# When the next tile's weights are split: the split of w1 put ahead of the second product, that of w2 one part of the first product earlier

## The chip, the cores and the metric

One of the eight cores of a Trainium2 chip runs the kernel. The metric is the device time of one execution in microseconds (us); of several executions the median counts. TensorE (PE in the rows, its weight loads PEld) multiplies matrices, VectorE (DVE), ScalarE (ACT) and GpSimd (POOL) work element by element, and SyncE (SP) issues transfers. Each engine executes its own instructions in the order in which the program gives them, and waits for others by semaphores.

## The reference

```python
def reference(r, k, v, w, u, moe..., moe2...):
    attn = _attn_ref(r, k, v, w, u)      # linear attention with a decay w, 4 x 8 heads, 768 steps, 48 wide
    x = attn as (3072 tokens, 384)
    # mixture of experts: each token goes to the expert with the largest logit
    logits = x @ w_gate + modality_bias[modality_id]
    e_idx = argmax(logits);  gate_w = softmax(logits)[e_idx]
    for e in range(8):
        h = maximum(x[mask] @ w1[e], 0)              # 384 -> 1024
        out[mask] = gate_w[mask] * (h @ w2[e])       # 1024 -> 384
    # a last network, the same for all tokens
    h = maximum(maximum(x @ w1, x @ w2), x @ w3)     # 384 -> 768
    return h @ w_out                                 # 768 -> 384
```

The decay w is drawn between 0.80 and 0.95. The modality bias is drawn with a spread of 0.5 for two modalities, so most tokens of a modality go to one expert.

## The kernel before, in words

The kernel has three stages. First the attention, over 24 tiles of 128 tokens, with the routing of each tile behind it. Then `first_block`: the expert layer, over 13 tiles of 256 tokens that are sorted by expert (the list `seq`: tiles 0 and 1, an extra tile X for what is left of the first expert, then tiles 2 to 11; `s` counts 0 to 12, and `EARLY` is 2, the place of X). Then `second_block`: the last network, on 512 tokens at a time.

All products are done with numbers in two parts. A value `a` is split into `ah`, its rounding to fp32r, and `al = a - ah`, and a product is the sum of three matmuls: high by high, low by high and high by low. In `mm3` these are lines 1143, 1144 and 1145; the third is the one that reads the low part of the weights (`w1l` or `w2l`). A split is one ACT instruction (line 502, the cast to `w1h` or `w2h`) and one subtraction (line 504) on DVE; for parts 1, 3, 4 and 6 of w2 the subtraction is on POOL (`W2_DVE = (0, 2, 5, 7)` names those on DVE).

One tile of the expert layer goes like this:

- `g1(q)`, q = 0 to 3: a quarter of the first product, 18 matmuls over 256 tokens for two blocks of 128 columns of `h` (three slices of the depth, three matmuls each), into one PSUM bank. ACT then writes `hh` (line 1156), DVE `hl` (line 1157). Blocks 0 to 3 use the weights that `split_w1` makes in parts 0 to 2, blocks 4 to 7 those of parts 3 to 5; each part is one of the three slices of the depth.
- behind each `g1(q)`, for s above 2, `split_w2` makes parts 2q and 2q+1 of w2, for the second product of the same tile.
- `reload(..., 1)`: SP loads the next tile's w2 into `w2r`, if that tile has another expert. It waits until the splits have read `w2r`.
- `next_columns`: PE transposes the next tile's tokens, ACT writes `xh` and DVE `xl` (lines 1136 and 1137).
- `rows_of` and `ids_of`: POOL clears buffers and issues the indirect transfers that fetch the tokens of the tile after the next.
- `g2(q)`, q = 0 and 1: the second product, 48 and then 24 matmuls; of the eight slices of the depth the last two come last. ACT copies each result to `raw` (line 1172). Behind each of the two, `split_w1` makes three parts of w1 of the next tile.
- `reload(..., 0)` loads w1 of the tile after the next, and `keep` writes `raw` to memory (SP, lines 1092 and 1176).

Between these calls `vw(n)` puts n steps of another job, which splits the weights of the last network: DVE lines 528 to 556, ACT lines 524 and 549, POOL lines 552 and 559 (`vh`, `vl`, `voh`, `vol`), loads on SP by line 517. `manual_schedule` leaves each engine with the order in which the code calls.

Line 495 is elsewhere: `check_w` counts over the 128 partitions those in which every decay w lay between 0.7 and 1.4 (a matmul with ones), and sets `badw` if the count is too small; `badw` then leads to a general attention that computes all again. Partitions 0 to 15 and 64 to 79 hold padding, which is set to 1.0.

Of the kernel before, what the change touches and what calls it, by code (L numbers as in the profile page):

```python
# [15 lines left out]
ALU = mybir.AluOpType  # L16
# [32 lines left out]
def kernel(ctx: ExitStack, tc: tile.TileContext, rkw_t, v_t, vrk, u, modality, w_gate, bias, w1, w2, v1, v2,  # L49
                              v3, v_out, out):  # L50
    nc = tc.nc
    PE, DVE, ACT, POOL, SP = nc.tensor, nc.vector, nc.scalar, nc.gpsimd, nc.sync
    B, NC, _, D, _, HP, _ = rkw_t.shape
# [16 lines left out]
    EARLY = 2  # L70
# [26 lines left out]
    lgps = lgpool.tile([128, 512], F32, name="lgps")  # L97


    def ct(shape, dt, name):  # L100
        return const.tile(shape, dt, name=name)
# [38 lines left out]
    badw = ct([128, 1], F32, "badw")  # L140
# [171 lines left out]
    def settle(a, b):  # L312

        POOL.memset(places[:, a:b], 0)
# [40 lines left out]
    def plan(es):  # L355
# [37 lines left out]
        end = t2("end")  # L393
        DVE.tensor_tensor_scan(out=end, data0=zero8, data1=co, initial=cgs, op0=ALU.add, op1=ALU.add)
        checked = check_w()
        next(checked)
        yield "X"
# [88 lines left out]
    def check_w():  # L486

        fl = small.tile([128, 1], F32, tag="fl", name="fl")
        DVE.tensor_reduce(out=fl, in_=flag, axis=AX.XY, op=ALU.max)
        good = small.tile([128, 1], BF16, tag="good", name="good")  # L490
        DVE.tensor_scalar(out=good, in0=fl, scalar1=0.0, scalar2=None, op0=ALU.is_equal)
        yield
        PE.matmul(lgps[:, 272:273], lhsT=ones_bf, rhs=good, start=True, stop=True)
        yield
        DVE.tensor_scalar(out=badw, in0=lgps[:, 272:273], scalar1=2.0 * D, scalar2=None, op0=ALU.is_lt)
        yield
        DVE.tensor_copy(ctl[:, 62:63], badw)

# [770 lines left out]
    ex = Experts()  # L1269
# [41 lines left out]
    def ids_of(j):  # L1311
        for half in range(2):
            ex.gather_ids(T[j]["oi"][half], idxm[:, 2 * j + half:2 * j + half + 1])

    def rows_of(s):
        ex.room(s)
        for half in range(2):
            ex.gather(s, half)
# [10 lines left out]
    def go(n):  # L1329
        for _ in range(n):  # L1330
            next(work, None)

    def until(what):
        for got in work:
            if got == what:
                return

    def first_block(vw):

        seq = T[0:EARLY] + [X] + T[EARLY:]  # L1340
        tile_of = list(range(EARLY)) + [None] + list(range(EARLY, N))
        def next_columns(nx):
            for q in range(2):
                ex.x_part(nx, q)
        for s, cur in enumerate(seq):
            nx = seq[s + 1] if s <= N - 1 else None
            for q in range(4):
                if s == 0 and q < 2:
                    continue
                if s == 0:  # L1350
                    ex.g1((q,), lambda: go(FIRST_GO[2 * q - 3]))
                else:
                    ex.g1((q,))
                if s > EARLY:
                    ex.split_w2((2 * q, 2 * q + 1))
                    vw(V_OPS[3] if s == EARLY + 1 else V_OPS[4][q])
                elif s < EARLY:
                    if s == 0:
                        if q == 2:
                            ex.split_w2((6, 7), W2_FIRST)  # L1360
                        go(FIRST_GO[2 * q - 2])
                    if s:
                        go(6)
                if s == EARLY:
                    vw(V_OPS[2])
            if s == EARLY - 1:
                until("X")
                settle(NG, NTILE)
                for half in range(2):
                    ex.gather_ids(X["oi"][half], idxx[:, half:half + 1])  # L1370
                rows_of(X)
                until("rows")
                ids_of(EARLY)
                rows_of(T[EARLY])
                until("end")
                ids_of(EARLY + 1)
            if s >= EARLY and nx:
                ex.reload(tile_of[s + 1], 1)
            if not nx:
                second_start()  # L1380
            if nx and nx is not X:
                next_columns(nx)
            if s >= EARLY and s + 2 <= N:
                rows_of(seq[s + 2])
            if s >= EARLY and s + 3 <= N:
                ids_of(tile_of[s + 3])
            for q in range(2):
                ex.g2(cur, (q,))
                if nx is X and q == 0:
                    next_columns(X)  # L1390
                if s >= EARLY:
                    if nx:
                        ex.split_w1(range(3 * q, 3 * q + 3))
                elif s == 0:
                    go(6)
                if EARLY - 1 <= s:
                    vw(V_OPS[s] if s <= EARLY else V_OPS[6])
            if EARLY <= s + 1 <= N - 1:
                ex.reload(tile_of[s + 2], 0)
            if cur is not X:  # L1400
                ex.keep(cur, tile_of[s])
        m = maskx.rearrange("p (t a) -> p t a", a=2)[:, EARLY:]
        DVE.copy_predicated(oi_all.rearrange("p (t a) c -> p t a c", a=2)[:, EARLY:],
                            m.unsqueeze(3).to_broadcast([128, N - EARLY, 2, 2]),
                            oe.unsqueeze(1).to_broadcast([128, N - EARLY, 2, 2]))

    def second_start():
        ex.open_second(2 * TW)
        ex.x2(ex.fetch(0, 2 * TW))
# [52 lines left out]
    with tc.manual_schedule():  # L1462
        wes = ExitStack()
        ex.open_first(wes)
        e = NTILE

        hooks = {(13, "mid"): [chosen, bind(first_load, 0, 0)],
                 (14, "end"): [first_room],
                 (e - 2, "uterm"): [first_x, bind(ex.split_w1, (0, 1, 2))],
                 (e - 2, "late"): [bind(ex.split_w1, (3, 4, 5), "h")],  # L1470
                 (e - 1, "uterm"): [bind(ex.split_w1, (3, 4, 5), "l"), bind(ex.g1, (0,)),
                                    bind(ex.split_w2, (0, 1), W2_FIRST)],
                 (e - 1, "mid"): [bind(ex.split_w2, (2, 3), W2_FIRST)],
                 (e, "mid"): [bind(ex.g1, (1,), rest_of_routing)],
                 (e, "end"): [bind(ex.split_w2, (4, 5), W2_FIRST)]}
        for q in range(1, 7):
            hooks[(13 + q, "mid")] = [bind(first_load, q // 3 if q < 6 else 1, q if q < 3 else q - 3)]
        attention(hooks)
        pools["mm"] = pool(ctx, "mm", 4, space=PSUM)
        wres = pool(ctx, "wres", 1)  # L1480
        vh = [wres.tile([128, KD, F2], F32R, name=f"vh{i}") for i in range(3)]
        vl = [wres.tile([128, KD, F2], F32R, name=f"vl{i}") for i in range(3)]
        voh = wres.tile([128, KF2, DM], F32R, name="voh")
        vol = wres.tile([128, KF2, DM], F32R, name="vol")
        with ExitStack() as es:
            vw = v_stream(pool(es, "stage", 2))
            first_block(vw)
            second_block(vw)
        wes.close()
        rest()  # L1490
# [50 lines left out]
```

## Time and profile before

| | |
|---|---|
| time, median of 3 runs | 766.49 us (760.2 to 769.64) |
| the profiled execution | 770.97 us, its span 769.3 us, mean granted clock 0.948 |
| PE busy | 720.2 us (94%), PEld 642.9 us |
| DVE, ACT, POOL busy | 494.0 us (64%), 318.7 us (41%), 363.8 us (47%) |
| attention and routing, with the first expert tile | about 0 to 222 us |
| expert tiles from the first `raw` copy on | 222.3 to 450.4 us |
| last network | 450.4 to 769.3 us |

Busy shares are of the span. A matmul's duration in a row is longer than the distance to the next one, since matmuls are pipelined: of successive matmuls the difference of their start times tells what each costs.

### The profile page before, as it was taken

The numbers are of one execution on the slowest core, as the hardware profiler recorded it, in microseconds if no ns is written. First come the engines' busy times: TensorE is split into PE (matmuls) and PEld (weight loads), VectorE is DVE, ScalarE is ACT, GpSimd is POOL, SyncE is SP. The second block draws the span as 40 slices with busy tenths as digits, with TensorE's granted clock in tenths as the row PEclk, the third lists the DMA queues.
The fourth block names the chain that finished last, engine by engine and source line by source line (L and its number), as shares of the span: only waits on it lengthen the run. The fifth ranks groups of instructions, "written<-read, shape, count | busy, mean of one in ns | idle before, by whom it ended". The sixth has DMA issues, their size and how long they took to land.

```text
span 769.3 us, 13303 instructions
## 1 busy us (share of the span) xinstructions
PE 720.2 (94%) x4909; PEld 642.9 (84%) x4910; DVE 494.0 (64%) x929; ACT 318.7 (41%) x698; POOL 363.8 (47%) x388
## 2 busy tenths in 40 slices
PE   6899888889999999999999999999999999999991
PEld 3788767777899989999999987988988889889881
DVE  4899996996786998888888889424143142242320
ACT  5475645554333656566566633211212112122210
POOL 8699868898746667666764435110200101002011
PEclk8699989878599999999999999999999999999996
DMA  9899989993013322122235232020200200001000
GB/s 240 203 249 252 214 173 232 269 273 121 22 50 104 84 65 82 62 65 81 63 118 183 83 124 84 6 77 1 83 0 3 82 0 32 11 0 42 1 21 25
DMA packets 32383, 74.59 MB, mean 97 GB/s; under 512 B 5974, under 2 KB 19062, under 8 KB 32309
## 3 DMA queue, kind: packets, MB, share of 16 engines
q1 hardware_dynamic: 27508, 64.15, 30.5%
q0 software_dynamic: 4800, 9.49, 4.0%
q8 instruction: 41, 0.67, 0.4%
q14 instruction: 34, 0.27, 0.1%
HBM read 87.96 MB, written 14.38 MB: 133 GB/s over the span
## 4 chain that ended last, share of the span: by engine, by line
issue 37%; PE 30%; DVE 12%; DMA 8%; POOL 7%; ACT 2%; POOLq 0%; SPq 0%; DVEq 0%; ACTq 0%
DMA tq<-in_rkw_t_dram 6%; PE mm L1145 6%; PE mm L1144 5%; PE mm L1143 5%; PE yb L805 4%; POOL out_dram L1228 3%; DVE w1l L504 3%; PE mm L775 2%; PE yb L811 2%; DMA vt<-in_v_t_dram 1%; POOL w2l L504 1%; PE tp L788 1%; PE tp L706 1%; PE tp L859 1%; DMA w2r<-in_moe_w_dram 1%
## 5 line engine op out<-in xcount | busy, mean ns | idle before, releaser
L1208 DVE TENSOR_TENSOR w2r<-mm,w2r 128x512 f32<-128x512 f32 x72 | 49.7, 690 | 150.2 <-PE mm L1145 150.1
L1228 POOL DMA_INDIRECT out_dram<-w2r,oi_all x24 | 26.0, 1084 | 250.2 <-ACT w2r L1227 249.6
L1143 PE MATMUL mm<-w1h,vh 128*128 128x512 f32 x324 | 128.2, 396 | 0.9 <-DVE w2r L1208 0.9
L1145 PE MATMUL mm<-w1h,vl 128*128 128x512 f32 x324 | 128.2, 396 | 0.0
L1144 PE MATMUL mm<-w1l,vh 128*128 128x512 f32 x324 | 128.1, 395 | 0.0
L1145 PE MATMUL mm<-hh,w2l 128*128 128x256 f32 x312 | 89.3, 286 | 2.0 <-DVE w2l L504 1.0
L1144 PE MATMUL mm<-hl,w2h 128*128 128x256 f32 x312 | 88.5, 284 | 1.0 <-DVE hl L1157 1.0
L1143 PE MATMUL mm<-hh,w2h 128*128 128x256 f32 x312 | 89.2, 286 | 0.0
L1145 PE MATMUL mm<-xh,w1l 128*128 128x256 f32 x300 | 85.9, 286 | 2.2 <-DVE w1l L504 2.2
L1143 PE MATMUL mm<-xh,w1h 128*128 128x256 f32 x300 | 85.0, 283 | 0.0
L1144 PE MATMUL mm<-xl,w1h 128*128 128x256 f32 x300 | 84.8, 283 | 0.0
L1210 ACT CAST w2h<-w2r 128x512 fp32r<-128x512 f32 x36 | 22.3, 621 | 139.3 <-DVE w2r L1208 139.3
L1143 PEld LDWEIGHTS mm<-w1h,vh 128*128 128x128 f32 x324 | 60.9, 188 | 15.7 <-DVE w2r L1208 1.3
L1145 PEld LDWEIGHTS mm<-w1h,vl 128*128 128x128 f32 x324 | 60.9, 188 | 14.7
L1144 PEld LDWEIGHTS mm<-w1l,vh 128*128 128x128 f32 x324 | 60.9, 188 | 14.4
L504 POOL TENSOR_TENSOR w2l<-w2r,w2h 128x384 fp32r<-128x384 f32 x44 | 49.7, 1136 | 41.6 <-ACT w2h L502 39.1
L504 DVE TENSOR_TENSOR w1l<-w1r,w1h 128x512 fp32r<-128x512 f32 x66 | 51.8, 838 | 23.8 <-ACT w1h L502 23.7
L1145 PEld LDWEIGHTS mm<-hh,w2l 128*128 128x128 f32 x312 | 59.7, 191 | 3.9 <-DVE w2l L504 2.6
L805 PE MATMUL yb<-nat,am 128*128 128x56 f32 x384 | 53.1, 297 | 8.6 <-DVE lh L834 5.0
L1144 PEld LDWEIGHTS mm<-hl,w2h 128*128 128x128 f32 x312 | 59.7, 191 | 1.5 <-DVE hl L1157 1.4
L1145 PEld LDWEIGHTS mm<-xh,w1l 128*128 128x128 f32 x300 | 57.5, 192 | 4.1 <-DVE w1l L504 4.1
L1143 PEld LDWEIGHTS mm<-hh,w2h 128*128 128x128 f32 x312 | 59.8, 192 | 0.0
(252 smaller groups left out, 1728.0 us busy)
## 6 DMA issues: line engine op xcount, KB each, us to landing
w1r<-in_moe_w_dram SPq DMA_DIRECT2D x10, 1536.0 KB, 7.0
w2r<-in_moe_w_dram SPq DMA_DIRECT2D x10, 1536.0 KB
nat<-in_vrk_dram SPq DMA_DIRECT2D x24, 608.0 KB, 10.1
tq<-in_rkw_t_dram SPq DMA_DIRECT2D x46, 288.0 KB, 8.7
stg<-in_moe_w_dram SPq DMA_DIRECT2D x18, 384.0 KB, 3.1
vt<-in_v_t_dram SPq DMA_DIRECT2D x24, 192.0 KB, 6.6
x2t<-raw SPq DMA_DIRECT2D x12, 384.0 KB, 2.3
w1r<-x2t SPq DMA_DIRECT2D x12, 384.0 KB, 3.9
```

What stands on the lines that cost most here:

```text
L504: eng.tensor_tensor(out=lo, in0=src, in1=hi.bitcast(F32), op=ALU.subtract)
L706: PE.matmul(ps, lhsT=s["vt"][:, q, :], rhs=wgb[:, q].rearrange("p h e -> p (h e)"), start=(q == 0), stop=(q == KD - 1))
L775: PE.matmul(ps[o][:, p * 128:(p + 1) * 128], lhsT=s["kt"][q, p, :], rhs=s["rt"][q, p, :], start=True, stop=True)
L788: PE.transpose(out=ps[:, p * 128:(p + 1) * 128], in_=s["kt"][:, p, :], identity=ident)
L805: PE.matmul(yb[:, h * DV:(h + 1) * DV], lhsT=s["am"][:, 4 * (h % 2) + h // 2, :], rhs=s["v"][:, h, :], start=(h == 0), stop=(first and h = ...
L811: PE.matmul(yb[:, 2 * p * DV:(2 * p + 2) * DV], lhsT=s["rt"][:, p, :], rhs=sbd[i % 2][:, p, :], start=False, stop=(p == HP - 1))
L1143: PE.matmul(oc, lhsT=wh[:, kk, sl], rhs=xh[:, kk, :], start=first and kk == 0, stop=False)
L1144: PE.matmul(oc, lhsT=wh[:, kk, sl], rhs=xl[:, kk, :], start=False, stop=False)
L1145: PE.matmul(oc, lhsT=wl[:, kk, sl], rhs=xh[:, kk, :], start=False, stop=last and kk == nk - 1)
L1208: DVE.tensor_tensor(out=hv, in0=o, in1=hv, op=ALU.max)
L1210: ACT.copy(self.h2h[:, c, :], hv)
L1228: ins = POOL.indirect_dma_start(out=out[:, :], out_offset=bass.IndirectOffsetOnAxis(ap=ids[q][:, 0:1], axis=0), in_=ob, in_offset=None, bo ...
```

## The change

In `first_block` three lines move. For s above 2, `split_w2` of parts 0 and 1 is called ahead of `g1(0)`, and behind `g1(q)`, q = 0 to 2, it makes parts 2q+2 and 2q+3; behind `g1(3)` it makes none. For s of 2 and above, all six parts of `split_w1` for the next tile are called in one piece ahead of `g2(0)`, behind `next_columns`, `rows_of` and `ids_of`. Besides, the bound in `check_w` goes from 2D = 96 to 127.5.

```diff
@@ check_w
-        DVE.tensor_scalar(out=badw, in0=lgps[:, 272:273], scalar1=2.0 * D, scalar2=None, op0=ALU.is_lt)
+        DVE.tensor_scalar(out=badw, in0=lgps[:, 272:273], scalar1=127.5, scalar2=None, op0=ALU.is_lt)
@@ first_block
         for s, cur in enumerate(seq):
             nx = seq[s + 1] if s <= N - 1 else None
+            if s > EARLY:
+                ex.split_w2((0, 1))
             for q in range(4):
...
                 if s > EARLY:
-                    ex.split_w2((2 * q, 2 * q + 1))
+                    if q < 3:
+                        ex.split_w2((2 * q + 2, 2 * q + 3))
                     vw(V_OPS[3] if s == EARLY + 1 else V_OPS[4][q])
...
             if s >= EARLY and s + 3 <= N:
                 ids_of(tile_of[s + 3])
+            if s >= EARLY and nx:
+                ex.split_w1(range(6))
             for q in range(2):
                 ex.g2(cur, (q,))
                 if nx is X and q == 0:
                     next_columns(X)
-                if s >= EARLY:
-                    if nx:
-                        ex.split_w1(range(3 * q, 3 * q + 3))
-                elif s == 0:
+                if s == 0:
                     go(6)
```

The order on PE does not change. ScalarE at the end of the tile s = 5, before (a name behind the arrow is what is read; `t_...` is a buffer of the job of the last network's weights):

```order
L1156 ACTIVATE hh<-mm 128x512
L502 CAST w2h<-w2r 128x384 x2
L1136 CAST xh<-tp 128x3x128 x2
L1172 COPY raw<-mm 128x512
L502 CAST w1h<-w1r 128x512 x3
L549 CAST vh_2615<-t_4074 128x384
L1172 COPY raw<-mm 128x256
L502 CAST w1h<-w1r 128x512 x3
L524 ACTIVATE lf<-stg 128x384
L1156 ACTIVATE hh<-mm 128x512
L502 CAST w2h<-w2r 128x384 x2
```

The same place, now:

```order
L1156 ACTIVATE hh<-mm 128x512
L1136 CAST xh<-tp 128x3x128 x2
L502 CAST w1h<-w1r 128x512 x6
L1172 COPY raw<-mm 128x512
L549 CAST vh_2615<-t_4078 128x384
L1172 COPY raw<-mm 128x256
L524 ACTIVATE lf<-stg 128x384
L502 CAST w2h<-w2r 128x384 x2
L1156 ACTIVATE hh<-mm 128x512
L502 CAST w2h<-w2r 128x384 x2
```

The six casts of w1 stood behind the two copies of the second product's result and stand ahead of both; two casts of w2 stand ahead of the first `hh` of the tile. VectorE at the same place, before:

```order
L1157 SCALAR_TENSOR_TENSOR hl<-mm,hh 128x512
L504 TENSOR_TENSOR w2l<-w2r,w2h 128x384
L1137 TENSOR_TENSOR xl<-tp,xh 128x3x128 x2
L504 TENSOR_TENSOR w1l<-w1r,w1h 128x512 x3
L545 TENSOR_SCALAR ya<-t_4074 128x384
L504 TENSOR_TENSOR w1l<-w1r,w1h 128x512 x3
L528 TENSOR_SCALAR ya<-stg 128x384
L1157 SCALAR_TENSOR_TENSOR hl<-mm,hh 128x512
L504 TENSOR_TENSOR w2l<-w2r,w2h 128x384
L532 TENSOR_SCALAR ya<-ya 128x384
L536 TENSOR_SCALAR ya<-ya 128x384
```

The same place, now:

```order
L1157 SCALAR_TENSOR_TENSOR hl<-mm,hh 128x512
L1137 TENSOR_TENSOR xl<-tp,xh 128x3x128 x2
L504 TENSOR_TENSOR w1l<-w1r,w1h 128x512 x6
L545 TENSOR_SCALAR ya<-t_4078 128x384
L528 TENSOR_SCALAR ya<-stg 128x384
L504 TENSOR_TENSOR w2l<-w2r,w2h 128x384
L1157 SCALAR_TENSOR_TENSOR hl<-mm,hh 128x512
L504 TENSOR_TENSOR w2l<-w2r,w2h 128x384
L532 TENSOR_SCALAR ya<-ya 128x384
L536 TENSOR_SCALAR ya<-ya 128x384
```

The six subtractions of w1 stand right behind `xl`, and each `hl` stands behind one subtraction of w2 more than before.

## Rows read from the trace of the kernel before

**Rows 1.** Windows (stretch, length, busy time (x instructions), PEclk, DMA share, GB/s)

```profile
255.00:450.40 195.40, 190.16 (x1547) 185.88 (x1546) 170.02 (x255) 119.59 (x252) 123.46 (x123) 1.00 0.28 87
450.40:769.30 318.90, 302.05 (x1406) 257.22 (x1404) 114.39 (x165) 69.73 (x113) 40.01 (x37) 0.98 0.11 34
```

**Rows 2.** Timeline of ACT (start, duration, line, operation): copies of the second product

```profile
222.33 0.59 ACT L1172 COPY raw<-mm 128x512 f32<-128x512 f32 x1 [5.05 <-PE mm L1145]
...
239.73 0.59 ACT L1172 COPY raw<-mm 128x512 f32<-128x512 f32 x1 [5.16 <-PE mm L1145]
...
258.32 0.59 ACT L1172 COPY xe<-mm 128x512 f32<-128x512 f32 x1 [0.53 <-PE mm L1145]
...
447.71 0.59 ACT L1172 COPY raw<-mm 128x512 f32<-128x512 f32 x1 [4.16 <-PE mm L1145]
```

**Rows 3.** Waits of PEld, 255 to 278 us (total, times, longest)

```profile
PEld mm L1145 <- DVE w1l L504: 1.0, 3, 0.7
PEld mm L1144 <- DVE hl L1157: 0.9, 1, 0.9
PEld mm L1145 <- DVE w2l L504: 0.3, 1, 0.3
```

**Rows 4.** Waits of PEld, 278 to 430 us

```profile
PEld mm L1145 <- DVE w1l L504: 3.1, 7, 0.8
PEld mm L1145 <- DVE w2l L504: 1.7, 4, 0.8
PEld mm L1145 <- POOL w2l L504: 1.2, 2, 0.7
```

**Rows 5.** Waits of PEld, 430 to 450.3 us

```profile
PEld mm L1144 <- DVE hl L1157: 0.5, 1, 0.5
PEld mm L1145 <- DVE w2l L504: 0.5, 2, 0.3
```

**Rows 6.** Timeline of PE where the first product of s = 6 begins

```profile
318.54 0.28 PE L1143 MATMUL mm<-xh,w1h 128*128 128x256 f32 x1
318.66 0.28 PE L1144 MATMUL mm<-xl,w1h 128*128 128x256 f32 x1
319.22 0.39 PE L1145 MATMUL mm<-xh,w1l 128*128 128x256 f32 x1 [0.28 <-DVE w1l L504]
319.44 0.28 PE L1143 MATMUL mm<-xh,w1h 128*128 128x256 f32 x1
```

**Rows 7.** Timeline of ACT in the same tile

```profile
310.58 0.85 ACT L1136 CAST xh<-tp 128x384 fp32r<-128x384 f32 x2
315.86 0.59 ACT L1172 COPY raw<-mm 128x512 f32<-128x512 f32 x1 [4.43 <-PE mm L1145]
316.34 1.66 ACT L502 CAST w1h<-w1r 128x512 fp32r<-128x512 f32 x3
```

**Rows 8.** Timeline of DVE in the same tile, and two tiles later

```profile
313.71 1.01 DVE L1137 TENSOR_TENSOR xl<-tp,xh 128x384 fp32r<-128x384 f32 x2
317.00 3.37 DVE L504 TENSOR_TENSOR w1l<-w1r,w1h 128x512 fp32r<-128x512 f32 x3 [2.28 <-ACT w1h L502]
...
354.68 1.90 DVE L504 TENSOR_TENSOR w1l<-w1r,w1h 128x512 fp32r<-128x512 f32 x3 [2.99 <-ACT w1h L502]
```

**Rows 9.** Timeline of POOL in the same tile

```profile
317.57 1.03 POOL L559 TENSOR_TENSOR vl<-lf,t 128x384 fp32r<-128x384 f32 x1
```

**Rows 10.** Waits of DVE, 278 to 430 us

```profile
DVE w1l L504 <- ACT w1h L502: 20.4, 8, 3.5
```

**Rows 11.** Timeline of PE in the second product of s = 3

```profile
274.26 0.39 PE L1144 MATMUL mm<-hl,w2h 128*128 128x256 f32 x1 [0.69 <-DVE hl L1157]
```

**Rows 12.** Chain of waits (start, duration): the one load of w2 in it

```profile
408.18 7.41 DMA w2r<-in_moe_w_dram
```

**Rows 13.** Timeline of ACT at the end of the tile of that load

```profile
413.43 0.37 ACT L1172 COPY raw<-mm 128x256 f32<-128x256 f32 x1 [0.73 <-PE mm L1145]
```

**Rows 14.** Windows: the start of the last network (columns as Rows 1)

```profile
450.40:480.00 29.60, 28.73 (x125) 22.84 (x124) 25.08 (x43) 10.28 (x20) 14.00 (x13) 1.00 0.39 121
```

## The prediction

> **What bounds the kernel now.** I read the windows first. From 255 to 450 us, the stretch of the expert tiles that the edit touches, PE is busy 190.2 of 195.4 us at a granted clock of 1.00 [rows 1], so the matmuls set the pace and only what PE loses between them can be won. The edit removes and adds no instruction: it can give back waits of PE or make new ones. So the question is how large those waits are and who ends them.
>
> Their size comes from the copies of the second product's result, one per tile, which ACT makes the moment PE is done. Between the first two, 17.40 us, PE does 144 matmuls and waits for nothing (no split of this block stands there). The next distance, 18.59 us, has two sets of transposes more, (18.59 - 17.40) / 2 = 0.6 us a set [rows 2]. From the copy at 258.32 to that at 447.71 lie ten tiles, nine with one set and the last with none: without waits 9 x 18.0 + 17.4 = 179.4 us, in fact 189.4 [rows 2]. **About 10.0 us are lost over the ten tiles**, and this is the most that the edit can win here, 1.3%.
>
> Who ends them is told by PE's weight loads, which wait for the low parts: 1.0 + 0.9 + 0.3 us [rows 3], 3.1 + 1.7 + 1.2 us [rows 4] and 0.5 + 0.5 us [rows 5], 9.2 us in 21 waits. Each wait costs a little more, since the pipeline restarts: behind a wait the next matmul starts 0.22 us later (319.22 to 319.44) instead of 0.12 (318.54 to 318.66) [rows 6]. 9.2 + 21 x 0.10 = 11.3 us, near the 10.0 counted by tiles; I scale by 10.0 / 11.3 below.
>
> **The change, part by part.**
>
> *w1 ahead of the second product.* Before, the first three casts of w1 start behind the copy of the second product's first half, at 316.34 in the tile shown, though ACT had done `xh` by 311.43 and stood idle for 4.43 us [rows 7]. DVE, done with `xl` at 314.72, stands 2.28 us for the first cast, and its three subtractions then take until 320.4, while PE wants the first at 318.78 [rows 8, 6]. DVE stands like this in eight tiles for 20.4 us [rows 10]. Now the casts follow `xh` at once: six at 1.66 / 3 = 0.55 us end at 311.4 + 3.3 = 314.7, ahead of the copy due at 315.86, so the copy and the PSUM bank behind it are not late. The subtractions follow `xl`: three by 314.7 + 1.9 = 316.6, six by 318.5 (1.90 us for three, undisturbed [rows 8]), and PE's first need, 318.78, is met with over 3 us to spare for the first of them. The wait on w1 from 278 us on goes: 3.1 us in 7 waits, 3.8 with the restarts [rows 4].
>
> *w2 one part earlier.* The casts and subtractions of every part come one `g1` earlier, 18 x 0.12 = 2.2 us, and DVE has also lost the standing ahead of w1. The waits on w2 from 278 us on are 1.7 + 1.2 + 0.5 us in 8 [rows 4, 5], 4.2 with restarts, each at most 0.8: less than the shift. I count them gone.
>
> *The first of these tiles.* Between 255 and 278 us PE waits three times on w1, once on w2 and once on `hl`, 2.2 us, 2.7 with restarts [rows 3]. The last, `hl` at 274.26 [rows 11], is set by DVE, which has the densest part of the other weights' splits there. If the earlier waits go, PE only arrives earlier at this one. I count nothing won.
>
> *hl.* Each `hl` now has one more subtraction of w2 ahead of it on DVE. In the later tiles the 20.4 / 8 = 2.5 us that DVE no longer stands cover it; if they did not, the wait would be like the one at 274.26. The one wait on `hl` at the end, 0.5 us [rows 5], I leave in.
>
> *Transfers.* SP's order stays. The loads of w1 and w2 wait for the splits to have read the buffers, so they go out earlier by 2 us or more, and that of w2 is also needed earlier, by about as much: ahead of `g1(0)`. Only one load of w2 shows in the chain, 408.18 to 415.59 [rows 12], where ACT is free for the first cast of w2 at 413.8 [rows 13]. Unmoved it would hold ACT for 1.8 us, and with it the first `hh`, which PE needs only 8.6 us (72 x 0.12) later: nothing. POOL's fetches of tokens stand behind one subtraction fewer, and are used a tile later. They cost nothing either.
>
> *The bound of 127.5.* One instruction with another constant: nothing, as long as all 128 partitions count as good. The decays are drawn from 0.80 to 0.95 and the padding is 1.0, all inside 0.7 to 1.4.
>
> **The sum.** 3.8 + 4.2 = 8.0 us by the waits, times 10.0 / 11.3 = 7.1. I take 6.5, leaving about one wait in ten, since DVE and POOL still run over 60% of the time here [rows 1]. Against the profiled execution, 770.97 - 6.5 = 764.5 us. That execution is 4.5 us above the median of the runs, 766.49; the edit's gain does not depend on that, so the forecast is 766.5 - 6.5 = **760.0 us**, 0.8% faster.
>
> *A rule to weigh against it.* In the tile shown the three subtractions of w1 took 3.37 us, with POOL's subtraction of `vl` at 317.57 beside them, and 1.90 us where POOL did none: 1.47 us for one meeting [rows 8, 9]. The Trainium skill's page "SBUF — State Buffer", section "Who interferes with whom", says that a DVE instruction with two inputs in SBUF and a GpSimd instruction that reads SBUF exclude each other, and whichever is second waits for the whole of the other. By that rule, which these rows bear out, six such subtractions in one piece have more chances to meet POOL than three. It is a rival below; in the sum, POOL stands at its memsets and fetches during this piece, and I count at most one meeting, which the 3 us to spare take in.
>
> **The rivals.**
>
> *A, the pieces collide, and w1 stays late (0.12).* If POOL meets the run of subtractions twice ahead of the third one, they end at 314.7 + 1.9 + 2 x 1.47 = 319.5, behind the need at 318.78 [rows 6, 8, 9]. Then only w2 is won, 4.2 x 10.0 / 11.3 = 3.7 us: 762.8. Against: POOL's work on the other weights waits for DVE's, which stands behind the run.
>
> *B, given back in the last network (0.13).* The splits of the other weights have as many steps as before but less time until 450 us, and DVE is busy 25.1 of the first 29.6 us there [rows 14]. If that start is DVE's, the 6.5 us come back as waits on `vl`: 766.5. Against: PE is busy 28.7 of those 29.6 us [rows 14], so DVE does not set the pace there.
>
> *C, `hl` becomes late in every tile (0.05), and it gets slower.* A wait like that at 274.26 [rows 11] costs 0.9 us [rows 3] and 0.10 for the restart, 1.0 us. It comes where DVE ends the third `hl` later than 13 x 0.12 = 1.6 us into the second product. With two a tile over nine tiles: 18 x 1.0 - 7.1 = 10.9 us slower, 777.4. It turns the sign from one such wait a tile on. Against: the 2.5 us a tile of DVE's standing [rows 10] are more than one subtraction.
>
> *D, the change does not do what it says (0.01).* If fewer than 128 partitions count as good, the general attention and all expert tiles are computed again: at least another 195 us [rows 1], over 960 us.
>
> **How the numbers follow.** The forecast has 0.69: gains between 4 and 10 us, 756.5 to 762.5. Runs of one kernel spread over 760.2 to 769.6, so I let 2 to 3 us of scatter in at the lower end and take in A and B above: **753.5 to 767**. C and D lie outside. A difference of 2%, 15 us, is what a measurement can tell from no change. Not even all the 10.0 us reach it, so faster by over 2% has only scatter, 0.04; slower by over 2% has D and scatter on top of C, 0.03; within 2% the rest, 0.93.
>
> **What would show it.** In the changed profile, from 255 to 450 us: waits of PE and PEld on `w1l` gone from 278 us on, those on `w2l` near nothing; DVE's standing for the cast of w1, 20.4 us, mostly gone; copies of the second product still the moment PE is done; nine tiles near 18.0 us and the one after X still above 20; the last network as long as before, 318.9 us. Waits on `hl` in every tile would make C right, waits on `w1l` with long subtractions A, more idle PE after 450 us B.

## The result, and the profile after

The changed kernel takes **758.98 us** (median of 20 runs, 754.67 to 767.12) against 766.12 us (20 runs, 760.2 to 773.18). The ratio is 0.9917, 95% interval 0.9892 to 0.9942: 0.8% faster, within 2%. The ratio leaves out the few runs that lie over 1.5% above the fastest of their kernel, so it is not quite that of the medians. Forecast were 760.0 us and 0.8%.

The profiled execution has a span of 755.3 us, 14.0 less than before. Not all of that is the edit's. The windows of the changed kernel are cut at three events, which the profile before has too: the first copy of the second product's result, the transposes made in X for the tile behind it, the first matmul of the last network (stretch, length, busy times of PE, PEld, DVE, ACT and POOL, granted clock, DMA share, GB/s).

```profile
0.00:212.60 212.60, 185.32 (x1688) 159.29 (x1690) 189.91 (x430) 118.43 (x312) 183.96 (x209) 0.90 0.78 203
212.60:243.10 30.50, 29.91 (x248) 29.47 (x248) 20.46 (x75) 9.03 (x18) 15.02 (x18) 1.00 0.33 97
243.10:436.46 193.36, 189.99 (x1574) 189.52 (x1573) 170.58 (x262) 121.07 (x255) 128.52 (x125) 0.99 0.29 90
436.46:755.30 318.84, 302.08 (x1406) 257.24 (x1404) 113.93 (x165) 69.74 (x113) 39.53 (x37) 0.98 0.10 34
```

The third line is where the moved lines act: 193.36 us, against 198.67 before (from 251.71, where these transposes began, to 450.38). I call this **the stretch**. It has lost 5.3 us. The last network is unchanged, 318.84 against 318.9 us [rows 1]. The first line is the attention, where only the bound of 127.5 differs: 212.6 us at a clock of 0.90. In the profile before it took 222.3 us, at 0.85:

```profile
0.00:222.30 222.30, 195.25 (x1688) 167.19 (x1690) 184.85 (x430) 118.65 (x312) 183.13 (x209) 0.85 0.76 195
```

That part varies from one execution to the next, and the clock with it: further profiles of the changed kernel, below, reach the same transposes at 247.1 and 252.5 us, with before's at 251.7, and in the second of them the attention takes 223.1 us at 0.84.

The waits of PEld in the stretch, which were 9.2 us in 21 [rows 3 to 5], are these, all ahead of 275 us:

```profile
PEld mm L1144 <- DVE hl L1157: 3.8, 2, 2.3
```

From 275 us on there is none, on w1, w2 or `hl`: every tile behind lasts 17.93 us. How w1 is in time is seen in the tile s = 4. ACT in the changed kernel:

```profile
285.09 0.86 ACT L1136 CAST xh<-tp 128x384 fp32r<-128x384 f32 x2
285.82 3.24 ACT L502 CAST w1h<-w1r 128x512 fp32r<-128x512 f32 x6
290.95 0.59 ACT L1172 COPY raw<-mm 128x512 f32<-128x512 f32 x1 [1.90 <-PE mm L1145]
```

and DVE:

```profile
287.26 1.01 DVE L1137 TENSOR_TENSOR xl<-tp,xh 128x384 fp32r<-128x384 f32 x2
288.19 3.69 DVE L504 TENSOR_TENSOR w1l<-w1r,w1h 128x512 fp32r<-128x512 f32 x6
291.80 0.50 DVE L536 TENSOR_SCALAR ya<-ya 128x384 int32<-128x384 int32 x1
```

The six casts take 3.24 us, ACT then waits 1.90 us for PE, so the copy is not late [rows 7]; the subtractions follow `xl` without a pause, end at 291.88, and the next tile's first matmul that reads them starts at 293.87, where PE used to wait [rows 6, 8]. DVE now waits elsewhere. Its waits from 275 to 420 us:

```profile
DVE hl L1157 <- ACT hh L1156: 12.8, 9, 3.0
DVE w2l L504 <- ACT w2h L502: 6.0, 6, 2.1
```

Before, it waited 20.4 us for the casts of w1 [rows 10] and then ran behind in the first product. Now it stands ready for `hh` and `w2h`: it runs ahead of what feeds it.

The two waits that are left fall in the tile behind X, s = 3, in its second product. PE there:

```profile
262.48 0.28 PE L1143 MATMUL mm<-hh,w2h 128*128 128x256 f32 x1
264.89 0.38 PE L1144 MATMUL mm<-hl,w2h 128*128 128x256 f32 x1 [2.13 <-DVE hl L1157]
...
265.58 0.28 PE L1143 MATMUL mm<-hh,w2h 128*128 128x256 f32 x1
267.10 0.58 PE L1144 MATMUL mm<-hl,w2h 128*128 128x256 f32 x1 [1.24 <-DVE hl L1157]
267.48 0.42 PE L1145 MATMUL mm<-hh,w2l 128*128 128x256 f32 x1
267.69 0.41 PE L1143 MATMUL mm<-hh,w2h 128*128 128x256 f32 x1
```

Here is the wait of [rows 11], now twice and longer. And behind it matmuls come 0.21 us apart instead of 0.12. The windows of these moments (columns as above, the granted clock third from the end) say why:

```profile
262.50:267.10 4.60, 1.23 (x9) 0.82 (x8) 4.57 (x8) 2.81 (x7) 3.57 (x4) 0.98 0.01 4
267.10:270.30 3.20, 3.20 (x15) 3.20 (x16) 3.20 (x7) 2.96 (x7) 2.74 (x5) 0.50 0.57 143
270.30:280.00 9.70, 9.70 (x82) 9.70 (x82) 8.08 (x15) 5.09 (x11) 5.17 (x6) 1.00 0.36 115
```

Behind 4.60 us in which PE was busy for 1.23, TensorE's clock was granted at 0.50, 1.2 GHz, for 3.2 us, and 15 matmuls cost some 0.09 us more each, 1.4 us.

### The profile page after: what moved, and what is told of

Same layout as the page of the kernel before. It is cut to its first block, busy times and chain, and to the rows that moved or that the text cites. A ratio compares the mean times of both kernels' runs of the same rounds, so it can differ in the third digit from the quotient of the medians.

```text
span 755.3 us, 13287 instructions
## 1 busy us (share of the span) xinstructions
PE 707.3 (94%) x4909; PEld 635.5 (84%) x4910; DVE 494.9 (66%) x929; ACT 318.3 (42%) x698; POOL 367.0 (49%) x388
## 4 chain that ended last, share of the span: by engine, by line
issue 35%; PE 23%; DVE 4%; POOL 4%; ACT 1%; POOLq 0%; DMA 0%; DVEq 0%; ACTq 0%; SPq 0%
PE mm L1144 7%; PE mm L1145 7%; PE mm L1143 7%; POOL out_dram L1228 3%; DVE ya L536 1%; PE tp L1132 1%; DVE t L541 1%; DVE ya L532 1%; DVE ya L528 1%; POOL vl L559 0%; DVE t L556 0%; ACT w1h L502 0%; DVE hl L1157 0%; DVE w2r L1208 0%; DMA stg<-in_moe_w_dram 0%
## 5 line engine op out<-in xcount | busy, mean ns | idle before, releaser
L1143 PEld LDWEIGHTS mm<-xh,w1h 128*128 128x128 f32 x300 | 57.6, 192 | 0.5 <-ACT xh L1136 0.5
L1144 PEld LDWEIGHTS mm<-xl,w1h 128*128 128x128 f32 x300 | 57.6, 192 | 0.5 <-DVE xl L1137 0.5
```

Source lines behind the costliest of these rows:

```text
L1143: PE.matmul(oc, lhsT=wh[:, kk, sl], rhs=xh[:, kk, :], start=first and kk == 0, stop=False)
L1144: PE.matmul(oc, lhsT=wh[:, kk, sl], rhs=xl[:, kk, :], start=False, stop=False)
```

## The experiments

The open question was which of the two moves brings the gain, and why the tile behind X got slower. The stretch is given for each kernel from one profile; ratios are to the kernel before in the same session.

| kernel | median, before | ratio (95%) | stretch | tile behind X | end |
|---|---|---|---|---|---|
| before | | | 198.67 | 20.24 | 28.51 |
| the change | 758.98, 766.12 | 0.9917 (0.9892 to 0.9942) | 193.36 | 23.32 | 26.59 |
| bound alone | 767.55, 767.99 | 0.9979 (0.9947 to 1.0012) | 198.31 | 20.24 | 28.51 |
| w1 alone | 760.04, 767.99 | 0.9895 (0.9852 to 0.9939) | 190.88 | 20.09 | 27.32 |
| w2 alone | 773.48, 767.99 | 1.0064 (1.0034 to 1.0095) | 205.55 | 21.98 | 28.83 |
| X as before | 760.39, 767.99 | 0.9877 (0.9842 to 0.9913) | 193.50 | 21.97 | 26.60 |
| fewer steps in X | 754.72, 766.75 | 0.9845 (0.9817 to 0.9872) | 187.97 | 17.93 | 26.57 |
| w2 a tile later | 761.09, 766.75 | 0.9891 (0.9852 to 0.9930) | 192.90 | 22.86 | 26.59 |
| both of these | 755.84, 766.75 | 0.9845 (0.9817 to 0.9873) | 187.97 | 17.93 | 26.57 |

A tile is counted from the transposes made in it, which are those for the next tile, to the next transposes: the tile behind X has its own second product and the first product of the tile after it. The end goes from the last transposes to the last network.

### The bound alone

```diff
-scalar1=2.0 * D, scalar2=None, op0=ALU.is_lt)
+scalar1=127.5, scalar2=None, op0=ALU.is_lt)
```

> The kernel before with the bound of 127.5 alone. Theory T (the gain is the waits of PE taken out of the expert tiles): nothing changes; from the transposes of the first of these tiles to the first matmul of the last network 198.7 us as before (within 1), ratio 1.000 within its interval. Rival R (in the two profiles 9.7 of 14.0 us of the difference lie ahead of the edited lines, so the gain sits in the attention and comes with any edit or with the bound): the part up to the first copy of the second product's result takes about 213 us instead of 222, ratio near 0.99.

```profile
252.38:450.69 198.31, 193.20 (x1574) 189.12 (x1573) 172.35 (x261) 120.71 (x254) 124.39 (x125) 1.00 0.29 88
```

The stretch is as before, the ratio takes in 1, and the first copy comes at 223.0 us, as late as before (222.3; rival R said 213). The bound does nothing to the time that these runs can tell. That an edit further down shortens the attention is not shown either: the median less the stretch is 569.3 us for the kernel before, 569.2 for the bound alone, 569.2, 567.9 and 566.9 for the next three kernels. These differ by 2.4 us, and the stretch of one and the same code by 2.7 (below).

### w1 alone, and w2 alone

```diff
 # w1 alone: split_w1(range(6)) ahead of g2, as in the change
-            if s > EARLY:
-                ex.split_w2((0, 1))
...
-                    if q < 3:
-                        ex.split_w2((2 * q + 2, 2 * q + 3))
+                    ex.split_w2((2 * q, 2 * q + 1))
```

> Only the split of w1 moves, that of w2 stays where it was. T, both moves needed: waits on w1l gone (3.1 us of PEld from the third tile on), those on w2l (3.4 us) stay, the stretch of the expert tiles 194 to 196 us of 198.7, ratio 0.994 to 0.996. Rival S (the late subtractions of w1 were the cause of the late w2l and hl too, since DVE ran behind): w2l waits go as well, but for at most 1.2 us behind POOL, the stretch 192 to 194 us, ratio 0.991 to 0.993, as good as the whole change or better, since no hl stands behind one more subtraction.

```diff
 # w2 alone: split_w2 as in the change
-            if s >= EARLY and nx:
-                ex.split_w1(range(6))
...
+                if s >= EARLY:
+                    if nx:
+                        ex.split_w1(range(3 * q, 3 * q + 3))
```

> Only the split of w2 moves, that of w1 stays. T: w2l waits gone, w1l waits as before (4.1 us of PEld in 10), the stretch 195 to 197 us, ratio 0.995. Rival S (DVE runs behind because of w1's second half; one more subtraction ahead of each hl makes those late): w1l waits stay and waits on hl come in several tiles, 0.5 to 1 us each, the stretch 198 to 204 us, ratio 0.998 to 1.006.

PEld's waits in the stretch with w1 alone:

```profile
PEld mm L1144 <- DVE hl L1157: 1.3, 2, 0.9
PEld mm L1145 <- POOL w2l L504: 0.7, 1, 0.7
PEld mm L1145 <- DVE w2l L504: 0.5, 1, 0.5
```

and with w2 alone:

```profile
PEld mm L1144 <- DVE hl L1157: 12.4, 13, 2.2
PEld mm L1145 <- DVE w1l L504: 2.4, 9, 0.7
```

Rival S holds on both sides in kind, and each time goes further than its range (190.88 us where it said 192 to 194, 205.55 where it said 198 to 204). With w1 alone, the waits on w2 go as well, 3.7 us [rows 3 to 5] to 1.2, though w2 is split where it was: what made `w2l` late was DVE. Its waits in the stretch, before:

```profile
DVE w1l L504 <- ACT w1h L502: 23.7, 10, 3.5
DVE hl L1157 <- ACT hh L1156: 0.7, 1, 0.7
```

and with w1 alone:

```profile
DVE hl L1157 <- ACT hh L1156: 20.4, 10, 4.1
```

Before, DVE stood for the casts of w1 and then came to all `hl` but one, and to every subtraction of w2, when its input was there: it was behind. With w1 alone it stands about as long, but for `hh`: it is ahead. Whether the standing or the second three subtractions of w1, which had followed it, weighed more, no run separates. With w2 alone, the `w2l` waits go and 12.4 us of waits on `hl` come in their place: the stretch is 6.9 us longer, the kernel 0.6% slower. DVE's backlog is still there, and each `hl` now has one more subtraction ahead of it. The wait on which DVE loses most in that kernel is the old one:

```profile
DVE w1l L504 <- ACT w1h L502: 24.4, 10, 4.5
```

So the two moves do not add up: -7.8, +6.9, and together -5.3 to -8.0 us (below). Only the first makes the room on DVE that the second takes.

### The tile behind X

X has six steps of the other weights' split at each of six places, six in ten of them on DVE, and in the change all of w1's subtractions stand ahead of the last two of these places. Three kernels ask what makes `hl` late behind it.

```diff
 # X as before
-            if s >= EARLY and nx:
+            if s > EARLY and nx:
                 ex.split_w1(range(6))
...
+                if s == EARLY:
+                    ex.split_w1(range(3 * q, 3 * q + 3))
```

> The whole change but for the tile X: there w1 of the next tile is split in two threes behind the second product, as before. The changed kernel waits 3.8 us there for hl, and its clock is 0.50 for 3.2 us behind these waits. If the run of six subtractions ahead of the densest vector work makes hl late: the hl wait falls to 1 to 2 us, the w1l wait of 1.0 us comes back, the clock stays at 1.00, the stretch 190 to 192 us instead of 193.4. Rival: if the casts and subtractions of w2 ahead of hh and hl make it late, it stays at 3 to 4 us and the stretch is 194 to 195.

```profile
PEld mm L1144 <- DVE hl L1157: 2.5, 2, 2.3
PEld mm L1145 <- DVE w1l L504: 1.3, 3, 0.9
```

This is between the two expectations: PE still waits 2.5 us for `hl` (2.6 in a second profile of the change, below), the w1 wait is back, and nothing is won in the stretch, 193.50 us. The clock fell here too, to 0.50 (last section). The run of six is not the cause. (The ratio, 0.9877, is better than this stretch gives, 5.2 of 768 us; six runs and one profile leave that open.)

```diff
 # fewer steps in X
-V_OPS = (0, 7, 6, 2, (3, 2, 2, 0), 7, 3)
+V_OPS = (0, 7, 4, 2, (4, 3, 2, 0), 7, 3)
```

> The whole change, and in the tile X four instead of six steps of the other weights' split at each of six places; two more in each of the nine later tiles. If the load of DVE in X makes hl late in the tile behind it: its length falls from 23.3 us to 18 to 19, the clock stays at 1.00 there, the stretch of the expert tiles is 188 to 189.5 us instead of 193.4, ratio to the kernel before 0.986 to 0.988. Rival (the order hl behind w2l is what makes it late): the wait stays above 2 us, the stretch above 191. Second rival: two more steps a tile make hl late later on; the tiles there come out longer than 17.93 us.

```profile
246.02:433.99 187.97, 187.97 (x1574) 187.97 (x1573) 172.35 (x262) 121.98 (x255) 128.54 (x126) 1.00 0.30 93
```

PE is busy for all of the stretch; no engine's wait shows on it, and the later tiles, with two more steps each, stay at 17.93 us. It is the load of these steps in X that made `hl` late, and the later tiles had room for it. The edit takes steps of ACT and POOL out as well; that DVE is the engine is read from the windows of the change, in the section on the result, where it was busy for 4.57 of the 4.60 us in which PE waited twice. The kernel takes **754.72 us, ratio 0.9845 (0.9817 to 0.9872)**, and its runs spread least, 754.42 to 756.95.

```diff
 # w2 a tile later
-            if s > EARLY:
+            if s > EARLY + 1:
                 ex.split_w2((0, 1))
...
+                    if s == EARLY + 1:
+                        ex.split_w2((2 * q, 2 * q + 1))
-                    if q < 3:
+                    elif q < 3:
                         ex.split_w2((2 * q + 2, 2 * q + 3))
```

> The change, but in the first tile behind X the split of w2 stays behind each part of the first product; from the second on it is one part earlier. Theory: that tile is as with w1 alone (20.1 us against 23.3), the last as in the change (26.6 us from its transposes to the last network against 27.3): stretch 190.1 us, ratio 0.988 to 0.990. Rival (a tile's order acts on the next one, so the waits move on): the second tile behind X is over 18.5 us.

A miss: 22.86 us for that tile instead of 20.1, though up to the late `hl` the code is that of w1 alone. The rival did not come either, the second tile took 17.93. So profiles of equal code differ by 2.8 us in this tile, and the order of w2 cannot be judged from one.

> Both of the last two edits together: w2 in the first tile behind X as before, four steps instead of six in X. Theory: no wait of PE is left in the stretch, nine tiles of 17.93 us and 26.6 us for the end, 188.0 us, 10.7 us less than before; ratio 0.985 to 0.987. Rival: as good as with fewer steps alone (within 0.3 us), since without DVE's backlog the order of w2 in that tile does not matter.

```profile
248.24:436.21 187.97, 187.97 (x1575) 187.97 (x1574) 171.48 (x260) 122.15 (x255) 127.82 (x125) 1.00 0.31 93
```

Both hold, and the rival exactly: with the load taken out of X, w2's order in that tile no longer matters. (w1 alone with fewer steps in X was not run.)

### The same code again

The two profiles with a slow tile behind X where w1 is split in one piece, that of the change and that of w2 a tile later, had one thing in common. In the tile ahead of X, ACT's copy came late. The change, first profile, where the transposes begin at 229.81 us:

```profile
232.40 0.58 ACT L1172 COPY raw<-mm 128x512 f32<-128x512 f32 x1 [6.77 <-remote]
```

As what ended ACT's wait the profile names only "remote". I ran the change twice more, and w1 alone once more, one execution each (758.21, 765.87 and 757.82 us).

> The changed kernel once more, for a second profile. In its first profile and in that of the kernel with w2 one tile later, ACT made the copy of the second product's first half in the tile ahead of X 2.6 and 1.3 us after the transposes began (0.2 in the kernel before), and the two tiles behind took 41.2 and 40.8 us; with w1 alone, the copy on time, 38.0. If the order of w2 itself makes hl late: 40 us or more also where the copy is on time. Rival (the late copy did it): 38 to 39 us where it is on time, about 41 where it is late.

> The changed kernel a third time, for the same question: of the three profiles, do the two tiles behind X take 40 us or more whenever w2 is early, or only where the copy ahead of X is late?

> The kernel with w1 alone moved a second time: 38 us for the two tiles if the copy ahead of X is on time; over 40 if it is late and that is the cause; 38 in either case if only w2's order matters.

The first repeat, where the transposes begin at 234.92 us:

```profile
235.12 0.59 ACT L1172 COPY raw<-mm 128x512 f32<-128x512 f32 x1 [5.17 <-issue]
```

and the tile behind X in it:

```profile
265.02:285.68 20.66, 18.45 (x153) 18.05 (x152) 20.56 (x32) 14.40 (x31) 15.83 (x16) 1.00 0.26 78
```

The copy is 0.2 us behind the transposes, as before the change; the second repeat has it 0.5 behind and a tile of 21.14 us. The clock stays at 1.00 in both. The two tiles take 38.6 and 39.1 us, the stretch 190.7 and 191.2. With w1 alone it is 20.10 us again, 38.0 for the two, 190.9 for the stretch. So the rival explains most of it: a late copy goes with 2.1 to 2.8 us more over the two tiles (X and the tile behind it), in the first profile some 1.4 of them by the clock.

How the one leads to the other shows on DVE. Behind a late copy `xh` is late and with it `xl`, which starts 3.6 us behind the transposes in the first profile and 1.2 in the first repeat. So DVE comes later to the subtractions of w1 in X. In the first profile, where X's transposes begin at 243.10 us, and in the first repeat, where they begin at 247.09:

```profile
251.05 3.69 DVE L504 TENSOR_TENSOR w1l<-w1r,w1h 128x512 fp32r<-128x512 f32 x6
```

```profile
253.79 3.69 DVE L504 TENSOR_TENSOR w1l<-w1r,w1h 128x512 fp32r<-128x512 f32 x6
```

That is 7.95 and 6.70 us behind them. The later DVE is there, the longer the two tiles: with w2 early 41.2 us at 7.95, 39.1 at 7.21 (second repeat), 38.6 at 6.70; with w2 as before 40.8 at 7.97 (w2 a tile later) and 38.0 at 6.7 (w1 alone, twice); with fewer steps in X, 35.9 at 4.38 in either order. No run delays the copy alone, so this link is read from the traces.

The order of w2 itself costs 0.6 to 1.0 us there, and wins 0.7 at the end (26.59 against 27.32). And against the repeats, X as before comes out worse than against the first profile: its copy was on time and its two tiles took 41.4 us, where the change on time took 38.6 and 39.1. So w1 in one piece in X is a gain of some 2.3 to 2.8 us there, the fall of the clock taken in. What delays ACT in some executions stays open.

## Why the prediction was right

- **The size of what can be won**, 10.0 us over the tiles: right. The two kernels in which no wait is left have a stretch 10.7 us shorter than before.
- **The gain**, 6.5 us: right. The stretch is shorter by 5.3, 8.0 and 7.5 us in three profiles, the ratio gives 0.0083 x 766 = 6.4 us (4.4 to 8.3).
- **w1 ahead of the second product**, 3.8 us: the mechanism was right, the size too small. Alone it wins 7.8 us, since most of the waits on w2 hung on it as well; 1.3 of the 7.8 came in the first two tiles, where I had counted nothing.
- **w2 one part earlier**, 4.2 us: this step failed. I credited the waits on `w2l` to w2's own place. They came from DVE running behind, and w2's move alone costs 6.9 us. Beside w1 it is worth nothing that these runs can tell. That the sum came out was luck in this part: most of the 4.2 us were won, but by the other term.
- **The first of these tiles**, nothing won: right on the mechanism, `hl` set by DVE's load in X. With the copy on time the two tiles win 0.3 to 0.8 us (39.36 before); with the late copy they lose 1.9. That `hl` would be late twice there, and the clock fall behind it, I did not foresee.
- **hl in the later tiles**: right. The time that DVE no longer stood covered the extra subtraction; the wait at the end, which I had left in, went too. What did stay was the tile behind X, 2.6 to 3.8 us in two waits, more than the one wait in ten that I had left.
- **Transfers and the bound**: nothing, as forecast.
- **Rival A** did not come, though the meetings did. In eight of the ten tiles the six subtractions took 3.69 us or 3.68, as long as 1.90 for three [rows 8]: POOL's clears lay ahead of them and at most its fetches beside them. In the other two POOL worked on `vl` (an addition, line 559, not a subtraction) or `lf` beside them, in spite of my argument that this work stands behind the run. The six took 5.01 and 4.87 us there, 1.3 and 1.2 more, one meeting each as I had counted, and no weight load waited for `w1l`. The Trainium skill's page "SBUF — State Buffer" (section "Who interferes with whom") says that a DVE instruction with two inputs in SBUF contends with a GpSimd instruction that reads SBUF. The trace agrees with it in these two tiles.
- **B** did not come, 318.84 us. **C** did not come in the change but is what w2 alone does: one late `hl` or so a tile turned the sign, as its point of decision said.

One of the two meetings of rival A in the changed kernel:

```profile
359.39 5.01 DVE L504 TENSOR_TENSOR w1l<-w1r,w1h 128x512 fp32r<-128x512 f32 x6
362.81 1.03 POOL L559 TENSOR_TENSOR vl<-lf,t 128x384 fp32r<-128x384 f32 x1
```

## What to carry to other kernels

When PE waits for an operand, the instruction that makes it may only be the one that stands last in a queue that runs behind: look for what that engine waited for earlier, and move that first. Two moves that each look worth their waits need not add up, and each should be run alone. Where preparatory work is spread over stretches without regard to their room, take it from the stretch whose engine has none: here three numbers in a table of steps took out the last waits, 2.7 us and more beyond the change.

## What was not expected of the hardware

- The clock can fall behind short waits of PE in a stretch that is otherwise at full clock: behind 2.13 and 1.24 us of waiting within 4.6 us it was 0.50 for 3.2 us, 1.4 us lost on top. With X as before, behind one wait of 2.06 us, and with w2 a tile later, behind 1.46, 0.29 and 0.68 us, it fell too. In the repeats of the change, behind 0.97 and 1.24 us and behind 1.46 and 1.24 us, it stayed at 1.00. These runs do not tell the cases apart by the waits alone.
- The same code reached the same point of the program at 243.1, 247.1 and 252.5 us. A difference of 10 us in the spans of two profiles says nothing on an edit of 6 us; the length of the stretch that it touches says more, and even that came out at 193.4, 190.7 and 191.2 us for this one code.

The falls with X as before and with w2 a tile later, in windows:

```profile
270.90:274.30 3.40, 3.40 (x18) 3.40 (x17) 3.40 (x7) 3.40 (x8) 2.64 (x3) 0.50 0.55 167
```

```profile
274.60:278.10 3.50, 3.50 (x17) 3.49 (x17) 3.50 (x6) 3.50 (x9) 3.04 (x5) 0.52 0.27 96
```
